# Linear attention, soft mixture of experts and an ELU feed-forward in one kernel: the order and the engines of the weights' conversion, and of the feed-forward's first units, are changed

## The chip, the cores and the metric

The kernel runs on one core of a Trainium2 chip. The metric is the time of one launch in device microseconds (us): the median of repeated runs. The core's engines each work through an instruction queue of their own, in order: TensorE (PE: matrix products; PEld: its weight loads), VectorE (DVE), ScalarE (ACT), GpSimd (POOL) and SyncE (SP, which here only issues DMAs). Where one needs what another makes, it waits on a semaphore.

## The reference

Three layers follow one another. Shapes: batch 4, 8 heads, 768 steps, head size 48; so 3072 tokens of 384 values; 8 experts of 4 slots, hidden size 1024; feed-forward width 2048. `w_in` and `w_out` arrive as 64-bit floating point values; the kernel reads them as pairs of 32-bit words.

```python
for t in range(S):                                   # linear attention, per batch and head
    cur = einsum('bhd,bhe->bhde', u * k_t, v_t)
    y[:, :, t] = einsum('bhd,bhde->bhe', r_t, state + cur)
    state = w * state + einsum('bhd,bhe->bhde', k_t, v_t)
x = y as [3072, 384]
logits = x @ phi                                     # soft mixture of experts
slot_input = softmax(logits over tokens).T @ x
slot_out[e] = relu(slot_input[e] @ w1[e]) @ w2[e]
x = softmax(logits over slots) @ slot_out
h = x @ w_in                                         # feed-forward
out = where(h > 0, h, exp(min(h, 0)) - 1) @ w_out
```

## The kernel before

The program has three stages, and all three engines' orders are those in which the code is written (a manual schedule).

**Attention** works on 24 chunks of 128 tokens (6 per batch), in a loop over s = -2 to 23 in which the pieces of chunks s, s+1 and s+2 are interleaved. For the chunk ahead, `scale` makes `km` (DVE), `turn(0)` transposes r (PE into PSUM tile `ps_r`) and multiplies it by a table into `rT` (DVE), and `turn(1)` transposes `km` into `ps_k`, copies it to `kT` (ACT) and multiplies it by `rT` into `qd` (DVE): this is the "r x k" of the change. `scores` multiplies `kT` by `rT` (PE), `causal` masks the result into two tiles `am` (DVE, line 559), `update` and `state` carry the state forward (`t1` on DVE, then `qc` on POOL, line 583), `bonus_b` ends in `bv` (POOL, line 601), and `rows_b` makes the chunk's output `x` (DVE, line 635), which `x_T` transposes. `ps_r`, `ps_x` and `ps_k` share two PSUM buffers, so `ps_k` waits until DVE has read `ps_r` into `rT`. Pieces of the mixture's logits and slot sums (`part`, `extra`) lie between them, three chunks to a round.

In the same loop the first part of `w_in` and `w_out` is converted from 64 to 32 bits, a piece of 128 x 384 in each of 20 steps (s = 0 to 19): `wide_load` (SP), `wide_a` (two ACT instructions, lines 313 and 314), `wide_b1` (a clamp, line 317, on POOL in this loop), `wide_b2`, `wide_b3`, `wide_c` (DVE, lines 322, 328 and 333), and one step later `wide_d` (two POOL instructions, lines 336 and 337). The loop also issues the loads of the experts' weights (`load_we`), nine of them at a pace set by `(s - 2) * (NWE - 1) // (NP - 3)` (NWE = 10, NP = 20), and one at s = 20 into the buffer of the conversion.

**Experts**: `up`, `turn`, `down` on PE; `turn_c_b` copies the transposed softmax from PSUM to `cT` (12 ACT instructions); `split` cuts five pieces of `w_out` (`wo`) in a rounded part `wh` (ACT) and a remainder `wl` (DVE); `turn_so` and three DVE copies give `sT`.

**Feed-forward**: `through` multiplies `sT` by columns of `w_in` on PE into PSUM tiles `phm`; `through_b` copies half of such a result to `mst` (ACT) and writes the remainder (DVE). Then 48 units (a block of 512 tokens and two columns of 128 hidden values each) run through `hid` (PE, tile `fh`), `tanh` and `expo` (ACT), `neg` and `elu` (DVE), `upper` (ACT, `gh`), `lower` (DVE, `gl`) and `outp` (24 PE products into `fo`). The first four units go in halves (`narrow`).

```python
            wide(s, wide_a)
            wide(s, wide_b1)
...
                rows_b(s)
                wide(s, wide_b2)
                wide(s - 1, wide_d)
...
            wide(s, wide_b3)
            wide(s, wide_c)
            if ahead:
                turn(1, s + 2)
```

Of the kernel before, what the change touches and what calls it, by code (L numbers as in the profile page):

```python
# [236 lines left out]
def kernel(  # L237
# [75 lines left out]
        nc.scalar.activation(out=a.bitcast(F32), in_=raw[:, :, 1].bitcast(F32), func=ACTF.Abs)  # L313
        nc.scalar.activation(out=l.bitcast(F32), in_=l.bitcast(U32), func=ACTF.Copy, scale=2.0 ** -52)

    def wide_b1(raw, a, eng=None):
        (eng or nc.vector).tensor_scalar(  # L317
            out=a.bitcast(F32), in0=a.bitcast(F32), scalar1=EXP_LO, scalar2=EXP_HI, op0=ALU.max, op1=ALU.min
        )

# [76 lines left out]
    with ExitStack() as actx:  # L397
# [415 lines left out]
        def wide(j, f):  # L813
            if 0 <= j < NP:
                raw, a = piece(j)
                if f is wide_b1:
                    f(raw, a, nc.gpsimd)
                    return
                if f is not wide_d:
                    f(raw, a)  # L820
                    return
                merged = []
                for o, at, i, c, p, m in spans(j):
                    if merged and merged[-1][0] == o:
                        merged[-1][3] += m
                    else:
                        merged.append([o, at, p, m])
                for o, at, p, m in merged:
                    wide_d(raw[:, at:at + m, :], a[:, at:at + m], (wov if o else wiv)[:, p:p + m])
# [27 lines left out]
        for s in range(-2, NCH):  # L857
            now, nxt, ahead = s >= 0, 0 <= s + 1 < NCH, s + 2 < NCH
            last = s == NCH - 1
            if nxt:  # L860
                update(s + 1)
            wide(s, wide_a)
            wide(s, wide_b1)
            if last:
                extra()
                extra()
                extra()
                logits(GS - 1, 0, G - 1)
            else:
                extra()  # L870
            if s > 0 and s % G == 0:
                extras += part(s // G - 1)
            if s == -2:
                tables_b()
            if nxt:
                state(s + 1)
            if ahead:
                scale(s + 2)
            if 2 <= s + 4 < NCH:
                load_k(s + 4)  # L880
            if 2 <= s + 3 < NCH:
                load_v(s + 3)
            if s < 1:
                wide_load(s + 2)
            if now:
                for p in range(HP):
                    rows_a(s, p)
                rows_b(s)
                wide(s, wide_b2)
                wide(s - 1, wide_d)  # L890
                if s >= 1 and s + 2 < NP:
                    wide_load(s + 2)
            if nxt:
                for p in range(HP):
                    scores(s + 1, p)
                causal(s + 1)
                bonus_a(s + 1)
                bonus_c(s + 1)
            if not last:
                extra()  # L900
            if ahead:
                turn(0, s + 2)
            if 2 <= s + 4 < NCH:
                load_r(s + 4)
            if nxt:
                for p in range(HP):
                    before(s + 1, p)
            if now:
                x_T(s)
            if last:  # L910
                logits(GS - 1, G - 1, G)
            if nxt:
                bonus_b(s + 1)
            wide(s, wide_b3)
            wide(s, wide_c)
            if ahead:
                turn(1, s + 2)
            if nxt:
                state_b(s + 1)
            if s == NCH - 2:  # L920
                warm(3)
            extra()
            if s >= 2 and (s - 2) * (NWE - 1) // (NP - 3) >= nwe and nwe < NWE - 1:
                load_we(nwe, we_p)
                nwe += 1
            if s == NP:
                assert nwe == NWE - 1
                load_we(nwe, we_p)
                nwe += 1
            if s >= NCH - 3 and not last:  # L930
                h = s - NCH + 3
                (rk_ctx, early)[h].close()
                pool = w2ctx.enter_context(tc.tile_pool(name=f"we2a{h}", bufs=1, side="right", reuse_waits="tile"))
                we.setdefault(NWE, []).append(pool.tile([128, HW], F32, name=f"we2a{h}"))
                load_half(NWE, h)
                nwe = NWE + h
        last_part(GS - 1)
        assert not extras

# [107 lines left out]
    def turn_c_b(b):  # L1047
        ph = ph_p.tile([128, CG // 2, 128], F32, tag="ph", name="phc")
        t = cs.pop(b)
        for i in range(CG // 2):  # L1050
            nc.tensor.transpose(
                out=ph[:, i, :], in_=t[:, 2 * i:2 * i + 2].rearrange("p n a c -> p (n a c)").bitcast(F32), identity=ident
            )
        o = cT[:, 128 * CG * b:128 * CG * (b + 1)].rearrange("p (i n t) -> p i n t", n=2, t=128)
        for n in range(2):
            for a in range(2):
                nc.scalar.copy(out=o[64 * a:64 * a + 64, :, n, :], in_=ph[64 * n:64 * n + 64])


    pt = [po_p.tile([128, 64], F32, tag="po", name="pt") for kk in range(KD)]  # L1060
# [7 lines left out]

    def split(i):
        a, b = (t[:, 2 * i % 8:2 * i % 8 + 2, :] for t in whl[i // 4])  # L1070
        nc.scalar.copy(out=a, in_=wo[:, 2 * i:2 * i + 2, :])
        nc.vector.tensor_tensor(out=b, in0=wo[:, 2 * i:2 * i + 2, :], in1=a.bitcast(F32), op=ALU.subtract)

    up(0)
# [65 lines left out]


    phm = [fo_p.tile([128, 512], F32, tag="fo", name="phm") for _ in range(2)]
    m0 = through(0, 256, phm[0][:, 0:256])
    through_b(*m0, 0)
    m2 = through(1024, 128, phm[0][:, 256:384])
    through_b(*m2, 0)
    through_b(*m2, 1)
    through_b(*m0, 1)


    PB = 384
# [94 lines left out]
    def term(n, i, t, terms):  # L1246
# [1 line left out]
        first, final = (0, FA - 1) if f0 < FA else (FA, FT - 1)  # L1248
        f = f0 + i
        wh, wl = (w[:, f % 8, :] for w in whl[f // 8])  # L1250
        if f == first and 0 in terms:
            po[blk, t] = fo_p.tile([128, DM], F32, tag="fo", name="fo")
        o = po[blk, t]
        s = slice(128 * t, 128 * t + 128)
# [30 lines left out]
    def narrow(n):  # L1285
        u = n - 1
        neg(u, ta)
        if u:
            lower(u - 1, tb)
        elu(u, ta)  # L1290
        if u:
            tanh(n, ta)
        upper(u, ta)
        if not u:
            tanh(n, ta)
        neg(u, tb)
        expo(n, ta)
        lower(u, ta)
        elu(u, tb)
        tanh(n, tb)  # L1300
        upper(u, tb)
        if not u:
            through_b(*m1, 1)
        expo(n, tb)

    late = []
    hid(0)
    m1 = through(512, 256, phm[1][:, 0:256])
    for s in (ta, tb):
        tanh(0, s)  # L1310
        expo(0, s)
    through_b(*m1, 0)
    for n in range(1, N + 3):
        j, at = (n - 7) // 2, n - 2 if n < SHIFT else n - 3
        if n == 2:
# [5 lines left out]
            outp(at, (0,))  # L1321
        if n < N:
            hid(n)
        if n == 20:
            m = through(CA, CB // 2, fh_p.tile([128, 512], F32, tag="fh", name="phm2"))
            late += [(*m, 0), (*m, 1)]
# [77 lines left out]
```

## Time and profile before

| what | value |
|---|---|
| median of 3 runs (lowest, highest) | 467.81 us (466.58, 467.82) |
| the profiled execution | 467.28 us, of which the span of the profile is 465.5 us |
| busy over the span | PE 416.9, DVE 369.6, ACT 268.5, POOL 186.3 us |
| attention, 16.75 to 162.70 us of the span | PE 122.29, DVE 127.69, POOL 102.27 of 145.95 us |
| experts, 180 to 215 us | PE 32.54 of 35 us |
| feed-forward's start, 215 to 235 us | PE 15.83 of 20 us, at a granted clock of 0.83 |
| rest of the feed-forward, 260 to 465 us | PE 193.82 of 205 us |

Busy time alone says little: the four stages have different limits, so each stage is read by itself, by the instructions in order of time and by what ended each wait. Start times are counted from the start of the span. An instruction's row gives its start and its duration; where two of one engine follow without a wait, the second may start a little before the first ends, so that the distance from start to start is what one costs.

### The profile page before, as it was taken

Reading aid. Unit: us, or ns where it says so; the run is one execution under the profiler, and the core shown is the slowest. Engines: PE = TensorE matmul, PEld = TensorE weight load, DVE = VectorE, ACT = ScalarE, POOL = GpSimd, SP = SyncE. Lnnn points to the kernel's source line nnn. Section 1 sums busy time; section 2 is a strip of 40 time slices with the busy share of each in tenths; the row PEclk is TensorE's granted clock in tenths of the full one; section 3 lists DMA queues with packets and bytes.
Section 4 is the critical chain, followed back from the end, with each engine's and each line's share of the span. In section 5 each row is a group of like instructions: output and inputs, shape, how many; then the busy total and the mean of one; then the engine's idle time right before and its main releaser. Section 6 shows DMA issues by size and latency. Waiting matters only on the chain.

```text
span 465.5 us, 9991 instructions
## 1 busy us (share of the span) xinstructions
PE 416.9 (90%) x4009; PEld 365.4 (78%) x4009; DVE 369.6 (79%) x553; ACT 268.5 (58%) x487; POOL 186.3 (40%) x185
## 2 busy tenths in 40 slices
PE   7888788798879898995999899989999999999995
PEld 6777677676768774443899789969998989999994
DVE  4798889898988854454887999996999987787851
ACT  2444254345445332485677787867868686866740
POOL 2385667777777613200000245331234304324440
PEclk9999899999999999998899999999999999999999
DMA  9959989999999858850000111211111001111112
GB/s 127 214 124 273 232 211 252 259 281 261 277 233 244 228 200 271 294 182 0 2 1 0 34 35 35 67 36 35 34 35 34 1 0 51 36 52 68 70 70 73
DMA packets 97575, 57.41 MB, mean 123 GB/s; under 512 B 77808, under 2 KB 89328, under 8 KB 97520
## 3 DMA queue, kind: packets, MB, share of 16 engines
q1 hardware_dynamic: 96704, 56.64, 45.2%
q8 instruction: 33, 0.54, 0.5%
q14 instruction: 22, 0.18, 0.1%
q10 hardware_dynamic: 816, 0.05, 0.1%
HBM read 51.96 MB, written 4.72 MB: 122 GB/s over the span
## 4 chain that ended last, share of the span: by engine, by line
PE 50%; DVE 16%; POOL 13%; ACT 10%; issue 8%; DMA 3%; POOLq 0%; DVEq 0%; ACTq 0%; SPq 0%
PE fo L1256 12%; PE fo L1257 11%; PE fo L1259 11%; POOL scr L317 5%; PE fh L1211 3%; DVE ex L1230 3%; DVE ex L1225 3%; DMA scr<-in_moe_w_out_dram 2%; POOL scr L336 2%; PE ph L1011 2%; POOL bv L601 2%; DVE am L559 2%; ACT scr L313 1%; PE ps_a L554 1%; ACT th L1219 1%
## 5 line engine op out<-in xcount | busy, mean ns | idle before, releaser
L1256 PE MATMUL fo<-wh,gh 128*128 128x384 f32 x384 | 132.3, 344 | 7.0 <-ACT gh L1238 3.7
L1257 PE MATMUL fo<-wl,gh 128*128 128x384 f32 x384 | 130.7, 340 | 0.0
L1259 PE MATMUL fo<-wh,gl 128*128 128x384 f32 x384 | 122.2, 340 | 0.0
L1256 PEld LDWEIGHTS fo<-wh,gh 128*128 128x128 f32 x384 | 72.9, 190 | 14.0 <-ACT acc L1193 6.5
L1225 DVE SCALAR_TENSOR_TENSOR ex<-ex,th 128x1024 f32<-128x1024 f32 (+1 forms) x52 | 62.1, 1195 | 23.3 <-ACT ex L1222 23.1
L336 POOL TENSOR_TENSOR cv<-raw,cv 128x384 f32<-128x384 f32 x12 | 19.8, 1652 | 138.7 <-DVE cv L333 66.4
L1241 DVE TENSOR_TENSOR gl<-ex,gh 128x1024 fp32r<-128x1024 f32 (+1 forms) x52 | 72.0, 1385 | 3.5 <-ACT gh L1238 3.0
L1219 ACT ACTIVATE th<-fh 128x1024 f32<-128x1024 f32 (+1 forms) x53 | 50.3, 949 | 42.4 <-PE fh L1211 42.4
L1257 PEld LDWEIGHTS fo<-wl,gh 128*128 128x128 f32 x384 | 72.8, 190 | 1.9
L1259 PEld LDWEIGHTS fo<-wh,gl 128*128 128x128 f32 x384 | 72.2, 190 | 0.0
L1230 DVE SCALAR_TENSOR_TENSOR ex<-ex,fh 128x1024 f32<-128x1024 f32 (+1 forms) x52 | 58.8, 1131 | 0.1
L1222 ACT ACTIVATE ex<-fh 128x1024 f32<-128x1024 f32 (+1 forms) x53 | 50.3, 949 | 9.5 <-DVE gl L1241 9.4
L1238 ACT CAST gh<-ex 128x1024 fp32r<-128x1024 f32 (+1 forms) x52 | 51.5, 991 | 5.4 <-DVE ex L1230 4.2
L1198 POOL TENSOR_TENSOR acc<-os,acc 128x384 f32<-128x384 f32 x20 | 29.0, 1482 | 49.7 <-ACT os L1197 49.7
L317 POOL TENSOR_SCALAR scr<-scr 128x384 f32<-128x384 f32 x20 | 30.8, 1538 | 35.7 <-ACT scr L313 35.7
L522 PE MATMUL ps_k<-ident,km 128*128 128x128 f32 x96 | 15.9, 290 | 23.5 <-DVE rT L532 22.2
L646 ACT COPY xT<-ps_x 128x384 f32<-128x384 f32 x24 | 11.5, 479 | 38.6 <-PE ps_x L644 38.6
L1211 PE MATMUL fh<-cT,mst 128*128 128x512 f32 x96 | 31.0, 404 | 2.8 <-DVE ex L1230 2.8
L522 PEld LDWEIGHTS ps_k<-ident,km 128*128 128x128 f32 x96 | 10.4, 143 | 28.4 <-DVE rT L532 26.7
L527 ACT COPY kT<-ps_k 128x512 f32<-128x512 f32 x24 | 14.1, 587 | 30.4 <-PE ps_k L522 30.2
L559 DVE TENSOR_TENSOR am<-ps_a,mask 128x512 f32<-128x512 f32 x48 | 30.7, 678 | 0.9 <-PE ps_a L554 0.9
L554 PE MATMUL ps_a<-rT,kT 64*128 64x128 f32 x384 | 29.0, 292 | 0.6 <-DVE rT L532 0.6
(160 smaller groups left out, 729.0 us busy)
## 6 DMA issues: line engine op xcount, KB each, us to landing
we<-in_moe_w_dram SPq DMA_DIRECT2D x14, 768.0 KB, 7.6
we<-in_moe_w_dram SPq DMA_DIRECT2D x16, 512.0 KB, 6.4
rp<-in_r_dram SPq DMA_DIRECT2D x24, 192.0 KB, 4.7
rk<-in_k_dram SPq DMA_DIRECT2D x24, 192.0 KB, 4.9
vd<-in_v_dram SPq DMA_DIRECT2D x24, 192.0 KB, 5.2
out_dram<-acc SPq DMA_DIRECT2D x24, 192.0 KB, 1.9
we<-in_moe_w_dram SPq DMA_DIRECT2D x16, 256.0 KB, 6.0
scr<-in_moe_w_out_dram SPq DMA_DIRECT2D x10, 384.0 KB, 5.1
```

The source lines that it names most:

```text
L317: (eng or nc.vector).tensor_scalar(out=a.bitcast(F32), in0=a.bitcast(F32), scalar1=EXP_LO, scalar2=EXP_HI, op0=ALU.max, op1=ALU.min)
L559: nc.vector.tensor_tensor(out=am[n, a], in0=aps[a], in1=mask.unsqueeze(1).to_broadcast([128, HP, 128]), op=ALU.mult)
L1211: nc.tensor.matmul(out=ph[n][:, i, :], lhsT=mst[(f + i) // 8][:, 128 * ((f + i) % 8):128 * ((f + i) % 8) + 128], rhs=cT[:, TB * blk:TB * b ...
L1219: nc.scalar.activation(out=th[n][:, s], in_=ph[n][:, s], func=ACTF.Tanh, scale=0.5)
L1222: nc.scalar.activation(out=ex[n][:, s], in_=ph[n][:, s], func=ACTF.Exp)
L1225: nc.vector.scalar_tensor_tensor(out=ex[n][:, s], in0=ex[n][:, s], scalar=1.0, in1=th[n][:, s], op0=ALU.add, op1=ALU.mult)
L1230: nc.vector.scalar_tensor_tensor(out=ex[n][:, s], in0=ex[n][:, s], scalar=0.0, in1=ph[n][:, s], op0=ALU.min, op1=ALU.max)
L1238: nc.scalar.copy(out=gh[n][:, s], in_=ex[n][:, s])
L1241: nc.vector.tensor_tensor(out=gl[n][:, s], in0=ex[n][:, s], in1=gh[n][:, s].bitcast(F32), op=ALU.subtract)
L1256: nc.tensor.matmul(out=o, lhsT=gh[n][:, i, s], rhs=wh, start=(f == first), stop=False)
L1257: nc.tensor.matmul(out=o, lhsT=gh[n][:, i, s], rhs=wl, start=False, stop=False)
L1259: nc.tensor.matmul(out=o, lhsT=gl[n][:, i, s], rhs=wh, start=False, stop=(f == final))
```

## The change

1. In the attention loop `wide_b1` (the clamp) goes from POOL to DVE and stands where `wide_b2` stood, behind `x`; `wide_b2` goes behind `bonus_b`, `turn(1)` (with `qd`) comes next, and `wide_b3` and `wide_c` follow it.
2. The loads of the experts' weights are paced over 20 steps instead of 17, the last one a step later.
3. In the experts' stage half of the `cT` copies go from ACT to DVE, and the `wh` copies from ACT to POOL.
4. At the feed-forward's start the first two `through` results lie in different PSUM tiles, `through_b` of the third comes later, one of its halves between DVE's instructions for unit 0, and 12 products of 128 x 384, whose result is overwritten, are added on PE ahead of the first `fo`.

```diff
-    def wide_b1(raw, a, eng=None):
-        (eng or nc.vector).tensor_scalar(
+    def wide_b1(raw, a):
+        nc.vector.tensor_scalar(
...
-                if f is wide_b1:
-                    f(raw, a, nc.gpsimd)
-                    return
...
             wide(s, wide_a)
-            wide(s, wide_b1)
...
                 rows_b(s)
-                wide(s, wide_b2)
+                wide(s, wide_b1)
                 wide(s - 1, wide_d)
...
                 bonus_b(s + 1)
+            wide(s, wide_b2)
+            if ahead:
+                turn(1, s + 2)
             wide(s, wide_b3)
             wide(s, wide_c)
-            if ahead:
-                turn(1, s + 2)
...
-            if s >= 2 and (s - 2) * (NWE - 1) // (NP - 3) >= nwe and nwe < NWE - 1:
+            if s >= 2 and (s - 2) * (NWE - 1) // NP >= nwe and nwe < NWE - 1:
...
-            if s == NP:
-                assert nwe == NWE - 1
-                load_we(nwe, we_p)
-                nwe += 1
+            if s == NP + 1:
+                load_we(NWE - 1, we_p)
...
-                nc.scalar.copy(out=o[64 * a:64 * a + 64, :, n, :], in_=ph[64 * n:64 * n + 64])
+                (nc.vector.tensor_copy if n else nc.scalar.copy)(
+                    out=o[64 * a:64 * a + 64, :, n, :], in_=ph[64 * n:64 * n + 64]
+                )
...
-        nc.scalar.copy(out=a, in_=wo[:, 2 * i:2 * i + 2, :])
+        nc.gpsimd.tensor_copy(out=a, in_=wo[:, 2 * i:2 * i + 2, :])
...
-    m0 = through(0, 256, phm[0][:, 0:256])
-    through_b(*m0, 0)
-    m2 = through(1024, 128, phm[0][:, 256:384])
-    through_b(*m2, 0)
-    through_b(*m2, 1)
-    through_b(*m0, 1)
+    m0 = through(0, 256, phm[1][:, 0:256])
+    m2 = through(1024, 128, phm[0][:, 0:128])
+    for i in range(2):
+        through_b(*m0, i)
+    for i in range(2):
+        through_b(*m2, i)
...
         neg(u, tb)
+        if not u:
+            through_b(*m1, 0)
         expo(n, ta)
...
-    m1 = through(512, 256, phm[1][:, 0:256])
+    m1 = through(512, 256, phm[1][:, 256:512])
...
-    through_b(*m1, 0)
...
+        if n == 1:
+
+            po[0, 0] = fo_p.tile([128, DM], F32, tag="fo", name="fo")
+            for i in range(12):
+                nc.tensor.matmul(
+                    out=po[0, 0], lhsT=whl[0][0][:, 0, :128], rhs=whl[0][0][:, 0, :], start=True, stop=True
+                )
```

How the instructions stand on DVE in one chunk of the attention loop, before:

```order
L635 TENSOR_TENSOR x<-py,bv 128x384
L322 TENSOR_SCALAR scr<-scr 128x384
L559 TENSOR_TENSOR am<-ps_a,mask 128x512 x2
L532 TENSOR_TENSOR rT<-ps_r,vt 128x512
L328 SCALAR_TENSOR_TENSOR scr<-scr 128x384
L333 TENSOR_SCALAR scr<-scr 128x384
L529 TENSOR_TENSOR qd<-rT,ps_k 128x512
```

and now:

```order
L635 TENSOR_TENSOR x<-py,bv 128x384
L317 TENSOR_SCALAR scr<-scr 128x384
L559 TENSOR_TENSOR am<-ps_a,mask 128x512 x2
L532 TENSOR_TENSOR rT<-ps_r,vt 128x512
L322 TENSOR_SCALAR scr<-scr 128x384
L529 TENSOR_TENSOR qd<-rT,ps_k 128x512
L328 SCALAR_TENSOR_TENSOR scr<-scr 128x384
L333 TENSOR_SCALAR scr<-scr 128x384
```

The clamp (L317) has taken the place of `wide_b2` (L322), which now stands between `rT` and `qd`; L328 and L333 have gone from ahead of `qd` to behind it.

POOL in one chunk, before:

```order
L317 TENSOR_SCALAR scr<-scr 128x384
L583 TENSOR_TENSOR qc<-t_149,w_141 128x192
L336 TENSOR_TENSOR scr<-scr 128x384
L337 TENSOR_TENSOR wo<-scr 128x384
L601 TENSOR_TENSOR bv<-vd,bs 128x384
```

and now:

```order
L583 TENSOR_TENSOR qc<-t_149,w_141 128x192
L336 TENSOR_TENSOR scr<-scr 128x384
L337 TENSOR_TENSOR wo<-scr 128x384
L601 TENSOR_TENSOR bv<-vd,bs 128x384
L583 TENSOR_TENSOR qc<-t_149,w_141 128x192
```

POOL's next instruction behind `bv` is now `qc`, which waits for DVE's `t1`; L336 and L337 (of the piece before) follow it at once.

DVE where the feed-forward starts, before:

```order
L1105 COPY sT<-pt 128x64 x3
L1139 TENSOR_TENSOR mst_3166<-phm,mst_3166 64x256
L1139 TENSOR_TENSOR mst_3167<-phm,mst_3167 64x128 x2
L1139 TENSOR_TENSOR mst_3166<-phm,mst_3166 64x256 x2
L1225 SCALAR_TENSOR_TENSOR ex<-ex,th 128x512
L1230 SCALAR_TENSOR_TENSOR ex<-ex,fh 128x512
L1225 SCALAR_TENSOR_TENSOR ex<-ex,th 128x512
L1241 TENSOR_TENSOR gl<-ex,gh 128x512
```

and now (its lines have moved by two):

```order
L1103 COPY sT<-pt 128x64 x3
L1137 TENSOR_TENSOR mst_3166<-phm,mst_3166 64x256 x2
L1137 TENSOR_TENSOR mst_3167<-phm,mst_3167 64x128 x2
L1223 SCALAR_TENSOR_TENSOR ex<-ex,th 128x512
L1228 SCALAR_TENSOR_TENSOR ex<-ex,fh 128x512
L1223 SCALAR_TENSOR_TENSOR ex<-ex,th 128x512
L1137 TENSOR_TENSOR mst_3166<-phm,mst_3166 64x256
L1239 TENSOR_TENSOR gl<-ex,gh 128x512
```

The third `through`'s first subtraction has gone from ahead of the first `neg` (L1225, now L1223) to behind the second one, ahead of `lower` (`gl`).

## Rows read from the trace of the kernel before

**Rows 1.** Busy time by stretch: start:end, us, then PE, PEld, DVE, ACT, POOL, PEclk, DMA share, GB/s
```profile
16.75:162.70 145.95, 122.29 (x2083) 103.36 (x2082) 127.69 (x242) 65.45 (x188) 102.27 (x100) 0.99 0.95 238
```

**Rows 2.** Waits of DVE, 16 to 163 us: total us, times, longest
```profile
DVE scr L322 <- POOL scr L317: 11.0, 10, 1.6
```

**Rows 3.** Order of time, DVE and POOL, one chunk: start us, us, engine, line
```profile
130.40 1.02 POOL L336 TENSOR_TENSOR scr<-scr 128x384 f32<-128x384 f32 x1
130.47 1.17 DVE L322 TENSOR_SCALAR scr<-scr 128x384 int32<-128x384 int32 x1 [1.32 <-POOL scr L317]
131.56 1.28 DVE L559 TENSOR_TENSOR am<-ps_a,mask 128x512 f32<-128x512 f32 x2
...
132.75 0.68 DVE L532 TENSOR_TENSOR rT<-ps_r,vt 128x512 f32<-128x512 f32 x1
133.35 0.54 DVE L328 SCALAR_TENSOR_TENSOR scr<-scr 128x384 int32<-128x384 int32 x1
...
133.93 0.36 DVE L333 TENSOR_SCALAR scr<-scr 128x384 int32<-128x384 int32 x1
...
134.85 0.69 DVE L529 TENSOR_TENSOR qd<-rT,ps_k 128x512 f32<-128x512 f32 x1 [0.56 <-ACT kT L527]
...
136.82 0.51 POOL L583 TENSOR_TENSOR qc<-t,w 128x192 f32<-128x192 f32 x1
136.89 0.65 DVE L322 TENSOR_SCALAR scr<-scr 128x384 int32<-128x384 int32 x1
```

**Rows 4.** Order of time, step s = 20: no clamp, but L336 follows `qc`
```profile
155.49 0.35 DVE L582 TENSOR_TENSOR t<-qc,pu 128x192 f32<-128x192 f32 x1
...
155.98 0.69 POOL L583 TENSOR_TENSOR qc<-t,w 128x192 f32<-128x192 f32 x1 [1.42 <-ACT c_sb L702]
156.22 0.55 DVE L635 TENSOR_TENSOR x<-py,bv 128x384 f32<-128x384 f32 x1
...
156.63 1.02 POOL L336 TENSOR_TENSOR scr<-scr 128x384 f32<-128x384 f32 x1
156.72 1.29 DVE L559 TENSOR_TENSOR am<-ps_a,mask 128x512 f32<-128x512 f32 x2
```

**Rows 5.** Order of time, DVE: output `x` of chunk 1
```profile
23.69 0.55 DVE L635 TENSOR_TENSOR x<-py,bv 128x384 f32<-128x384 f32 x1
```

**Rows 6.** Order of time, DVE in the feed-forward: the clamp on DVE, POOL idle
```profile
263.64 0.35 DVE L317 TENSOR_SCALAR cv<-cv 128x384 f32<-128x384 f32 x1
```

**Rows 7.** Order of time, end of the experts' stage; last row: POOL's clamp, ns min/median/max
```profile
204.60 1.80 PE L1033 MATMUL pd<-we,h1T 128*32 128x384 f32 x20
...
205.44 1.56 ACT L1071 CAST wh<-wo 128x768 fp32r<-128x768 f32 x2
...
207.03 0.58 ACT L1037 ACTIVATE so<-pd,rz 128x384 f32<-128x384 f32 x1
L317 POOL TENSOR_SCALAR scr<-scr x20: 1487/1505/1750, 16.7 to 149.3; 128x384 f32<-128x384 f32 x20
```

**Rows 8.** Order of time, feed-forward's start
```profile
212.32 0.26 ACT L1138 CAST mst<-phm 64x128 fp32r<-64x128 f32 x1 [1.43 <-PE phm L1129]
...
213.94 0.60 ACT L1219 ACTIVATE th<-fh 128x512 f32<-128x512 f32 x1
...
216.27 0.42 DVE L1139 TENSOR_TENSOR mst<-phm,mst 64x256 fp32r<-64x256 f32 x1 [1.90 <-ACT mst L1138]
216.72 0.69 DVE L1225 SCALAR_TENSOR_TENSOR ex<-ex,th 128x512 f32<-128x512 f32 x1
...
228.32 0.63 PE L1211 MATMUL fh<-cT,mst 128*128 128x512 f32 x2
```

**Rows 9.** Busy time by stretch in the feed-forward, columns as in rows 1
```profile
222.00:224.00 2.00, 2.00 (x7) 1.81 (x6) 1.97 (x4) 0.90 (x2) 0.00 (x0) 0.50 0.00 0
...
226.00:228.00 2.00, 2.00 (x14) 2.00 (x13) 1.91 (x4) 0.79 (x2) 0.00 (x0) 1.00 0.02 4
260.00:465.00 205.00, 193.82 (x1060) 184.91 (x1058) 172.28 (x171) 140.86 (x181) 69.27 (x43) 1.00 0.13 43
```

More of the change, by code (lines that the diff above doesn't have):

```diff
@@ L936 @@
                 nwe = NWE + h
+        assert nwe == NWE + 1
         last_part(GS - 1)
@@ L1250, in term @@
         wh, wl = (w[:, f % 8, :] for w in whl[f // 8])
-        if f == first and 0 in terms:
+        if f == first and 0 in terms and (blk, t) not in po:
             po[blk, t] = fo_p.tile([128, DM], F32, tag="fo", name="fo")
```

## The prediction

> **What bounds the kernel now.** I read the busy time by stretch first, to see which stages have one limit; then, stage by stage, the waits and the instructions in order of time. In the attention loop DVE is busy 127.69 of 145.95 us, ahead of PE and POOL [rows 1]. So 18.3 us of DVE are idle there, and 11.0 of these are waits of `wide_b2` (L322) for the clamp on POOL (L317) [rows 2]. What a chunk costs is a ring through DVE: `x`, L322, two `am`, `rT`; then PE's `ps_k` and ACT's `kT`; then `qd` and on to the next `x`. From the start of `rT` to the start of `qd` are 2.10 us (132.75 to 134.85), and L328 and L333 lie inside them: they cost nothing there, since `qd` would wait for `kT` anyway (0.56 us it still does) [rows 3]. The chunks' `x` come from 23.69 us (s = 1) [rows 5] to 156.22 us (s = 20) [rows 4]: 19 chunks of 6.98 us.
>
> One thing more is to be seen in rows 3. L322 takes 1.17 us where POOL's L336 started 0.07 us before it, and ends 0.22 us after L336 does; beside the short `qc`, which also started 0.07 us earlier, it takes 0.65. The same kind of instruction takes 0.35 us with POOL idle [rows 6]. So these DVE instructions wait until the POOL instruction that came first has ended. The Trainium skill says why on the page "SBUF — State Buffer", section "Who interferes with whom": DVE's two-port modes and GpSimd share a port pair, whoever issues first has it for the whole instruction, the other blocks. That speaks against giving DVE one more instruction of this kind; the trace agrees with it, by the 1.17 us.
>
> In the feed-forward PE is the limit, 193.82 of 205 us [rows 9], so a delay or a gain at its start lasts to the end.
>
> **The change, part by part**, against the profiled execution's 467.28 us (span 465.5 us; 0.5 us under the median of the runs).
>
> *Attention, per chunk.* L328 and L333 leave the 2.10 us, where they were free, and come behind `qd`: 0.58 us (133.35 to 133.93) and 0.36, in sum 0.94 us on the ring [rows 3]. POOL should be idle then, so I take the undisturbed durations. L322 goes into the 2.10 us in their place and costs nothing; were it to wait out a whole POOL instruction, as it waits out L336's 1.02 us in rows 3, it would still fit into the 1.5 us between the end of `rT` and `qd`. That takes off what it cost: 0.57 us beside `qc` in 16 chunks (0.65 less an overlap of 0.08), 1.09 beside L336 in 4 (130.47 to 131.56): 0.67 in the mean [rows 3]. The wait for POOL's clamp goes too: 11.0 us / 19 = 0.58 [rows 2].
>
> The clamp on DVE stands behind `x`. What does it meet? POOL's next work is `qc`, released by `t1`, and L336 at once behind it. Step s = 20 shows that order, without a clamp: `t1` starts at 155.49, `qc` 155.98, L336 at 156.63, and the DVE instruction behind `x` at 156.72 [rows 4]. The clamp would start there: 0.09 us behind L336, as L322 did with 0.07. So bounds for it are 0.35 us [rows 6] and 1.17 (1.09 from start to start) [rows 3], and I take 1.09, whose row has the same neighbours in the same order.
>
> Sum: 0.94 + 1.09 - 0.67 - 0.58 = +0.78 us a chunk. In 3 of the 19 chunks (the last but one of a batch, which have no `qc`) POOL begins earlier, and the clamp waits for L337's end instead: some 0.45 less each. 19 x 0.78 - 1.35 = 13.5 us. Of DVE's 18.3 us idle, 7.3 are not in the term of 11.0 [rows 1, 2]; some hang on POOL's clamp as well, and I let 3 of them go: **+10.5 us**. The 30 us that POOL loses (20 x 1.5 [rows 7]) gain nothing beyond the wait already counted.
>
> *Pace of the loads.* The queue is as full in bytes as before; two of the ten expert weights come a step or two later, and those are read by `down` only, which has all of `up` on PE before it. Cost nothing; without that cover one load of 1.57 MB at 238 GB/s [rows 1] would be 6.6 us.
>
> *Experts.* PE is continuous up to the end of `down(1)`, 204.60 + 1.80 = 206.40. ACT's `so`, which reads it, starts at 207.03, because two `wh` copies end at 207.00 [rows 7]. With the copies on POOL, `so` starts some 0.07 us behind PE: **-0.55 us**. POOL's price for a copy of 768 columns isn't shown. ACT's 0.78 is one end; twice the clamp's 1.5 us for 384 columns, 3.0, is the other [rows 7]. I take 1.5, nearer ACT's, since a copy has no arithmetic. Five are 7.5 us, and POOL has them all behind `up(1)`, 14 us ahead of `sT`: hidden at either end but for 1 us at the upper, where the last `wl` would come late for `sT`. The six `cT` copies that go to DVE lie beside PE's `down(1)`, where DVE has only `wl` to make; uncovered they would cost about six copies of the size of `so`, 6 x 0.58 = 3.5 us [rows 7].
>
> *Feed-forward's start.* ACT waits 1.43 us for PE's second `through` at 212.32, which waited until the first was read from the same PSUM tile, and the first `tanh` starts at 213.94 [rows 8]. In two tiles that wait goes, and `tanh` should start near 212.7, 1.2 us earlier. The first `neg` at 216.72 stood behind the third `through`'s subtraction at 216.27 [rows 8], and not behind `expo`; freed, it starts near 213.9, 2.8 us earlier. But that subtraction, 0.42 us and the wait for its ACT copy, now lies between `neg` and `lower`: it gives back about 1.2, and DVE's chain is 1.6 us earlier from there. Then the clock: it stood at 0.50 in 222 to 224, PE's 1.2 GHz level, and 7 products ran in 2 us; at the upper level 14 do [rows 9]. The 12 added products fill PE's empty time ahead of the first `fo`; at the upper level they take 1.7 us and end about when `gh` is there. If the clock holds, the 7 products to 224 cost 1 us instead of 2, and `hid` of unit 3 (228.32) comes 1.6 + 1.0 = 2.6 us earlier: **-2.6 us**. Ends: 0 (clock falls anyway, added products in the way) and -4.
>
> Sum: 467.3 + 10.5 - 0.55 - 2.6 = 474.6; I say **474.5 us**.
>
> **The rivals.** *The clamp comes first (faster).* If it has the port before L336, it costs 0.34 instead of 1.09 in the 16 chunks with `qc`: 16 x 0.75 = 12 us less, 462.5 us. The point that decides is the 0.09 us between L336 and the clamp [rows 4]. For it: it is small, and 0.69 us of `qc` there has slack in it (0.51 in rows 3). Against it: in rows 3 POOL won with 0.07 us, twice. The Trainium skill, page "Perfetto Trace Analysis", section "GPSIMD Engine Instruction", warns that a GpSimd span in a profile isn't reliable and that start-to-start spacing should be used; if so, when L336 takes the port is less sure than its row, and this rival would give its 462.5. The spacing agrees with the rows here (`qc` to L336, 0.65). *It is mixed:* the clamp wins in about half of the chunks, 474.5 - 6 = 468.5. *The feed-forward gives nothing:* the added products delay the first `fo`, or the clock falls in the gap behind it (PE should still wait there, for `gl` of unit 0): 477. For it: the clock did fall after an idle stretch in this place [rows 9].
>
> **How the numbers follow.** Forecast 0.52 (474.5), clamp first 0.27 (462.5), mixed 0.10 (468.5), no gain in the feed-forward 0.11 (477). Its own range, by the ends of -4 and 0 and by 3 us either way for the idle time that I let go: 471 to 478. Cases of both signs hold most of the chance, so the range goes on to the faster rival: 460.5 to 478. A measurement of this kernel tells 0.3%, 1.4 us, from no change. Faster: clamp first and a quarter of the mixed, 0.30. Same: 0.05. Slower: 0.65.
>
> **What would show it.** In the changed profile: chunk-to-chunk distance of `x` near 7.5 us (6.98 before), L317 on DVE at 1.1 to 1.2 us with L336 starting just before it, L322 hidden, L328 and L333 at 0.54 and 0.36; no DVE wait for POOL. `so` right behind `down(1)`; the clock at its upper level from `hid(0)` on; the distance from the first `tanh` to the end shorter by 1 to 2 us. Wrong if L317 on DVE has 0.35 us in most chunks (the first rival), or if the ring breaks elsewhere: L322 longer than the time for `kT`, or L328 and L333 made longer by a POOL instruction beside them.

## The result, and the profile after

The changed kernel takes 460.44 us (median of 4 runs, 458.81 to 462.65) against 467.19 of the kernel before in the same session: a ratio of 0.986, with an interval of 0.983 to 0.990. It is 1.4% faster; 474.5 us and slower was the forecast.

Where the 7.5 us between the two profiled executions (467.28 and 459.78 us; 7.4 of them inside the spans) lie is read from the start times of a few instructions:

| stretch | before | after | difference | forecast |
|---|---|---|---|---|
| start to `x` of s = 0 | 16.75 | 15.46 | -1.29 | 0 |
| 20 chunks, `x` of s = 0 to s = 20 | 139.47 | 135.83 | -3.64 | +10.5 |
| on to the first `sT` (last chunks, experts) | 51.97 | 51.75 | -0.22 | -0.55 |
| `sT` to `hid` of unit 3 | 20.13 | 17.99 | -2.14 | -2.6 |
| `hid` of unit 3 to the end of the span | 237.18 | 237.07 | -0.11 | 0 |

The experts and the feed-forward came out about as forecast; the attention loop went the other way, and the start moved, of which the forecast had nothing. Its busy times, in the columns of [rows 1], for the stretch that answers to them:

```profile
15.46:158.13 142.67, 126.15 (x2086) 103.52 (x2085) 127.64 (x263) 64.92 (x188) 72.48 (x80) 0.99 0.96 245
```

DVE has as much to do as before, 127.64 us, but in 3.3 us less (both stretches end with `x` of s = 21); the wait for POOL's clamp [rows 2] is gone. Now the waits, of DVE and then of PE (total us, times, longest), in the loop after:

```profile
DVE qd L529 <- ACT kT L527: 13.4, 17, 1.7
...
PE ps_k L522 <- ACT xT L646: 6.4, 14, 0.5
PE ps_k L522 <- DVE rT L532: 5.1, 6, 1.3
```

and PE's largest before:

```profile
PE ps_k L522 <- DVE rT L532: 22.2, 19, 2.3
```

Here is the surprise. Before, `ps_k` (the transpose of `k`, `turn(1)`) waited for DVE's `rT` in 19 chunks. After, it waits in 14 chunks for ACT's copy `xT` instead. By its data it needs neither. It waits for the reader of whatever last lay in its PSUM buffer. `ps_r`, `ps_k` and `ps_x` come from one pool, `pt_p`, with two buffers, and nothing in the code says which of the two a tile gets. In the program of before, `ps_k` follows `ps_r` in its buffer in 21 of the 23 chunks whose buffer held another tile before, and `ps_x` in one; in that of the change it follows `ps_x` in 14 and `ps_r` in 8. The lines that allocate these tiles are untouched: the assignment moved along with the order of the code.

One chunk of the change with `ps_x`'s buffer, in order of time (start us, us, engine, line):

```profile
102.96 0.55 DVE L635 TENSOR_TENSOR x<-py,bv 128x384 f32<-128x384 f32 x1
...
103.37 1.01 POOL L336 TENSOR_TENSOR scr<-scr 128x384 f32<-128x384 f32 x1
103.43 1.17 DVE L317 TENSOR_SCALAR scr<-scr 128x384 f32<-128x384 f32 x1
...
103.66 1.10 PE L612 MATMUL py<-qb,rT 128*128 128x96 f32 x8 [0.59 <-ACT bt L572]
...
104.59 0.49 PE L644 MATMUL ps_x<-ident,x 128*128 128x128 f32 x3
...
105.12 0.48 ACT L646 COPY xT<-ps_x 128x384 f32<-128x384 f32 x1 [1.04 <-PE ps_x L644]
...
105.66 0.66 PE L522 MATMUL ps_k<-ident,km 128*128 128x128 f32 x4 [0.46 <-ACT xT L646]
105.72 0.67 DVE L532 TENSOR_TENSOR rT<-ps_r,vt 128x512 f32<-128x512 f32 x1
...
106.32 0.48 DVE L322 TENSOR_SCALAR scr<-scr 128x384 int32<-128x384 int32 x1
106.40 0.59 ACT L527 COPY kT<-ps_k 128x512 f32<-128x512 f32 x1 [0.73 <-PE ps_k L522]
...
107.02 0.69 DVE L529 TENSOR_TENSOR qd<-rT,ps_k 128x512 f32<-128x512 f32 x1 [0.23 <-ACT kT L527]
...
107.63 0.55 DVE L328 SCALAR_TENSOR_TENSOR scr<-scr 128x384 int32<-128x384 int32 x1
...
108.21 0.36 DVE L333 TENSOR_SCALAR scr<-scr 128x384 int32<-128x384 int32 x1
...
109.39 0.55 DVE L635 TENSOR_TENSOR x<-py,bv 128x384 f32<-128x384 f32 x1
```

`ps_k` starts 0.06 us ahead of `rT`, and `rT` to `qd` is 1.30 us. The next chunk of the same trace has `ps_r`'s buffer:

```profile
112.15 0.67 DVE L532 TENSOR_TENSOR rT<-ps_r,vt 128x512 f32<-128x512 f32 x1
...
112.88 0.66 PE L522 MATMUL ps_k<-ident,km 128*128 128x128 f32 x4 [1.00 <-DVE rT L532]
...
113.63 0.59 ACT L527 COPY kT<-ps_k 128x512 f32<-128x512 f32 x1 [1.27 <-PE ps_k L522]
...
114.25 0.69 DVE L529 TENSOR_TENSOR qd<-rT,ps_k 128x512 f32<-128x512 f32 x1 [0.77 <-ACT kT L527]
...
117.10 0.55 DVE L635 TENSOR_TENSOR x<-py,bv 128x384 f32<-128x384 f32 x1
```

There `ps_k` waits 1.00 us for `rT`, and `rT` to `qd` is the 2.10 us of [rows 3]. The first chunk took 6.43 us from `x` to `x`, this one 7.71. Much else of the forecast is in the rows of the first chunk: the clamp starts 0.06 us behind L336 and takes 1.17 us (so it does in 11 of 20 chunks), L322 is hidden, L328 and L333 have 0.55 and 0.36.

For the experiments a chunk is cut in two: from the start of `x` to that of `qd`, where PE and ACT work beside DVE, and from `qd` to the next `x`, where L328 and L333 now stand. Sums over 20 chunks (s = 0 to 20), from the start times of `x` and `qd`, with DVE's busy time and the mean granted clock over the same stretch:

| kernel | `ps_k` shares with | `x` to `qd` | `qd` to `x` | sum, us | DVE busy | clock |
|---|---|---|---|---|---|---|
| before | `ps_r` in 21 of 23 | 104.68 | 34.79 | 139.47 | 123.22 | 0.99 |
| the change | `ps_x` in 14 of 23 | 84.50 | 51.33 | 135.83 | 123.11 | 0.99 |
| e1 the change | `ps_r` | 93.73 | 51.45 | 145.18 | 123.36 | 0.96 |
| e2 the change | `ps_x` | 81.81 | 51.33 | 133.14 | 123.14 | 1.00 |
| e3 before | `ps_x` | 99.09 | 34.62 | 133.71 | 120.45 | 0.99 |
| e4 e2, clamp early | `ps_x` | 87.96 | 62.53 | 150.49 | 113.66 | 0.91 |
| e5 e2, all steps behind `rT` | `ps_x` | 93.59 | 33.05 | 126.64 | 123.62 | 1.00 |
| e6 e5, clamp on POOL | `ps_x` | 104.54 | 32.76 | 137.30 | 133.97 | 1.00 |
| e9 e1, L328 and L333 put back | `ps_r` | 98.33 | 33.72 | 132.05 | 126.93 | 0.97 |
| e10 e1, clamp on POOL | `ps_r` | 82.11 | 56.00 | 138.11 | 116.88 | 0.96 |

### The profile page after: what moved, and what is told of

Same layout as the page of the kernel before. It is cut to its first block, busy times and chain, and to the rows that moved or that the text cites. A ratio compares the mean times of both kernels' runs of the same rounds, so it can differ in the third digit from the quotient of the medians.

```text
span 458.1 us, 10069 instructions
## 1 busy us (share of the span) xinstructions
PE 419.4 (92%) x4021; PEld 363.8 (79%) x4021; DVE 373.4 (82%) x579; ACT 260.7 (57%) x476; POOL 160.2 (35%) x170
## 4 chain that ended last, share of the span: by engine, by line
PE 61%; DVE 21%; issue 7%; ACT 7%; DMA 2%; SPq 1%; DVEq 0%; ACTq 0%
PE fo L1254 11%; PE fo L1257 11%; PE fo L1255 11%; PE fh L1209 3%; DVE ex L1228 3%; PE py L612 3%; PE ps_a L554 3%; DVE ex L1223 3%; PE ps_k L522 3%; PE py L625 3%; PE pd L1029 2%; PE ph L1007 2%; DVE am L559 2%; DVE km L517 2%; DVE scr L317 2%
## 5 line engine op out<-in xcount | busy, mean ns | idle before, releaser
L1223 DVE SCALAR_TENSOR_TENSOR ex<-ex,th 128x1024 f32<-128x1024 f32 (+1 forms) x52 | 62.1, 1194 | 24.1 <-ACT ex L1220 23.9
L336 POOL TENSOR_TENSOR cv<-raw,cv 128x384 f32<-128x384 f32 x12 | 19.5, 1624 | 132.3 <-DVE cv L333 59.8
L583 POOL TENSOR_TENSOR qc<-t,w 128x192 f32<-128x192 f32 x20 | 14.5, 723 | 59.9 <-DVE t L582 21.7
L529 DVE TENSOR_TENSOR qd<-rT,ps_k 128x512 f32<-128x512 f32 x24 | 16.5, 686 | 16.0 <-ACT kT L527 16.0
L554 PE MATMUL ps_a<-rT,kT 64*128 64x128 f32 x384 | 27.9, 285 | 0.3 <-ACT kT L527 0.2
L625 PE MATMUL py<-vd,am 128*64 128x48 f32 x768 | 27.3, 226 | 0.0
```

Of the source, the lines that this page charges most:

```text
L554: nc.tensor.matmul(out=aps[a][:, p, :], lhsT=kT[q, p, :], rhs=rT[n][q, p, :], start=True, stop=True)
L625: nc.tensor.matmul(out=py[q:q + 64, h, :], lhsT=am[n, a][:, p, q:q + 64], rhs=vd[n][:, h, :], start=(c == 0), stop=(c == 0 or h == H - 1),)
L1223: nc.vector.scalar_tensor_tensor(out=ex[n][:, s], in0=ex[n][:, s], scalar=1.0, in1=th[n][:, s], op0=ALU.add, op1=ALU.mult)
```

## The experiments

Theory A: the change gained because `ps_k` changed its buffer. Rival B: the new order gains whichever buffer `ps_k` has.

**e1, e2, e3: the buffer alone.** The first two are the change, the third is the kernel before. The edit of e1 leaves one buffer to `ps_r` and `ps_k`, and another to `ps_x`; e2 and e3 give `ps_k` the tag `px` too (tiles of one tag share a set of buffers).

```diff
-        pt_p = actx.enter_context(tc.tile_pool(name="pt_p", bufs=2, space=PSUM))
+        pt_p = actx.enter_context(tc.tile_pool(name="pt_p", bufs=1, space=PSUM))
...
-            ps = pt_p.tile([128, KD, 128], F32, tag="pt", name="ps_x")
+            ps = pt_p.tile([128, KD, 128], F32, tag="px", name="ps_x")
```

> The changed kernel with one edit: ps_r and ps_k share one PSUM buffer in every chunk (before the edit they do so in about 9 chunks of 23). Theory A (the change gained because ps_k got the bank of ps_x in 14 chunks, so that it no longer waited for rT): every chunk is then one of the 7.05 to 7.7 us kind instead of 14 of the 6.4 to 6.7 us kind, rT to qd is 2.1 us everywhere, and 14 x 0.8 us come back: 470 to 473 us. Rival B (the later steps' place behind r x k is what gains, whichever bank ps_k has): 459 to 462 us.

> The changed kernel with one edit: ps_k shares its PSUM buffer with ps_x in every chunk, so never waits for rT. Theory A: the 9 or so chunks that are left at 7.05 to 7.7 us fall to 6.4 to 6.7 us, 9 x 0.6 to 0.8 us less: 453 to 456 us, and no wait of ps_k for VectorE is left in the attention stage. Rival B: no change, 459 to 462 us. If the weight loads bound the stage (DMA share .96 of it), also no change, with x waiting for its transfer.

> The kernel before, with the one edit that ps_k shares its PSUM buffer with ps_x in every chunk. Theory A in its strong form (the bank alone is the gain): the 2 us between rT and qd fall to 1.3 us in each chunk, 458 to 460 us. Theory A in its weaker form (the freed 0.8 us is only there when the two later steps are out of that gap, since they take 0.9 us of VectorE in it): qd's own wait for kT goes, about 2 us in all, 464.5 to 466.5 us. Rival B: 467 us.

Measured: e1 473.09 us, 1.015 of before (1.012 to 1.018); e2 458.85 us, 0.985 (0.982 to 0.988); e3 461.63 us, 0.991 (0.988 to 0.994). PE's waits in e1 and then in e2:

```profile
PE ps_k L522 <- DVE rT L532: 20.0, 18, 2.6
```

```profile
PE ps_k L522 <- ACT xT L646: 10.1, 22, 0.5
```

Rival B falls with e1: the same instructions in the same order, with the buffer that `ps_k` had before, are slower than before. e1 lies 0.1 us above theory A's 470 to 473. Between e1 and e2 only the buffer differs, 14.2 us: in the traces e2 is 12.0 us shorter in the loop, 2.3 in the start, where e1 makes `ps_k` wait for `rT` from the first chunk on (the kernel before doesn't), and 1.5 behind `sT`, where the clock fell in e1, but 1.2 longer from s = 20 to `sT`. In e1's loop `ps_r` waits for no reader of `ps_k`, so that its new neighbour costs it nothing there. e2 gained less on the change than theory A said: 458.85 us is not in its 453 to 456, but just under rival B's 459. Of the 20 chunks counted, six have `ps_r`'s buffer in the change, and not nine; four of them give 0.5 to 1.1 us, two nothing. That is 2.7 us in the loop (135.83 to 133.14), 1.0 of it lost again in a later start; the two times can't be told apart. e3 lies between its two forms and gained more than the 2 us of the weaker one, 5.8 us in the loop: 2.5 of them between `rT` and `qd` (sums of 41.55 and 39.00), the rest ahead of `rT`, where the wait for POOL's clamp fell from 11.0 us to 8.9; why that fell wasn't followed up.

**e4: the clamp ahead of the state's instructions**, where POOL is idle, on e2:

```diff
+            wide(s, wide_b1)
             if nxt:
                 state(s + 1)
...
                 rows_b(s)
-                wide(s, wide_b1)
```

> As the run with ps_k behind ps_x, and the clamp of VectorE issued ahead of the state's instructions, where GpSimd is idle, so that it doesn't stand behind the sum on GpSimd. If the clamp's 1.17 us is the shared port's doing, it takes 0.35 us there, 0.5 to 0.8 us of each of 20 chunks less on VectorE: 443 to 450 us if VectorE still sets the chunk, and 451 to 456 us if TensorE (5.9 us of a chunk) or the loads do. If the clamp waits there for ScalarE's absolute value, the gain is smaller by that wait.

Measured: 477.16 us, 1.023 (1.019 to 1.027): 18 us slower than e2, though the clamp takes 0.35 us. In order of time:

```profile
115.13 0.55 DVE L635 TENSOR_TENSOR x<-py,bv 128x384 f32<-128x384 f32 x1
...
115.82 1.10 PE L612 MATMUL py<-qb,rT 128*128 128x96 f32 x8 [1.61 <-DVE x L635]
...
117.82 0.44 PE L522 MATMUL ps_k<-ident,km 128*128 128x128 f32 x2 [0.46 <-ACT xT L646]
...
119.19 0.69 DVE L529 TENSOR_TENSOR qd<-rT,ps_k 128x512 f32<-128x512 f32 x1 [1.32 <-ACT kT L527]
...
120.82 0.35 DVE L317 TENSOR_SCALAR scr<-scr 128x384 f32<-128x384 f32 x1
...
121.82 0.55 DVE L635 TENSOR_TENSOR x<-py,bv 128x384 f32<-128x384 f32 x1
```

In this chunk and in ten others `x` to `qd` is 4.05 to 4.07 us, as in most chunks of e2 and in the chunk of the change above: `x` frees `py`, then come L612, `ps_x`, `xT`, `ps_k` and `kT`, on PE and ACT. The long clamp stood beside that and cost nothing; the short one stands in `qd` to `x`, where DVE alone sets the pace, and there it also waits for ACT's absolute value (4.8 us in 7 chunks). Against e2 `qd` to `x` grows by 11.2 us in the 20 chunks. All cases of the expectation were gains; only the wait that it names at the end was there. The granted clock fell as well, to 0.83 in the mean from 40 to 80 us, where three chunks have 5.4 to 5.7 us from `x` to `qd`, and `x` to `qd` grows by 6.2 us in all; so the 18 us aren't the clamp's alone.

**e5, e6: all four DVE steps between `rT` and `qd`**, on e2 (the cut is e5's); in e6 the clamp stays where the change has it in the code, but on POOL, so behind `qc`:

```diff
                 rows_b(s)
-                wide(s, wide_b1)
...
+            wide(s, wide_b1)
             wide(s, wide_b2)
+            wide(s, wide_b3)
+            wide(s, wide_c)
             if ahead:
                 turn(1, s + 2)
-            wide(s, wide_b3)
-            wide(s, wide_c)
```

> ps_k in ps_x's bank in every chunk, and all of the conversion's VectorE steps (clamp and the three after it) between rT and qd. With that bank x to qd takes 4.06 us whatever VectorE does, because TensorE and ScalarE set it (x, state rows, ps_x, xT, ps_k, kT), and the two steps behind qd (0.91 us) lie in the other part, qd to x, which VectorE sets. Theory A (the chunk is these two parts in a row): x to qd stays at 4.1 to 4.3 us, qd to x falls from 2.36 to 1.45 us in a plain chunk, and 10 to 18 us of 20 chunks go unless TensorE's own sum (6.0 us of a chunk) ends it: 443 to 451 us. Rival C (the chunk is bound by the sum of VectorE's work, or by the loads at a DMA share of 1.0): 455 to 460 us.

> As the run with all steps between rT and qd, with the clamp on GpSimd, where it was before the change. Theory A: VectorE has slack between x and qd either way, so within 2 us of that run, unless bv comes late behind the clamp on GpSimd. Rival C (VectorE's sum): 20 clamps less on VectorE, 7 us faster than that run.

Measured: e5 455.95 us, 0.979 (0.975 to 0.982); e6 462.54 us, 0.991 (0.988 to 0.994). `qd` to `x` fell to 1.5 us in most chunks of e5, as expected, but `x` to `qd` rose to 4.55:

```profile
99.67 0.68 DVE L532 TENSOR_TENSOR rT<-ps_r,vt 128x512 f32<-128x512 f32 x1
...
100.27 0.48 DVE L317 TENSOR_SCALAR scr<-scr 128x384 f32<-128x384 f32 x1
...
100.78 0.36 DVE L322 TENSOR_SCALAR scr<-scr 128x384 int32<-128x384 int32 x1
100.79 1.04 POOL L601 TENSOR_TENSOR bv<-vd,bs 128x384 f32<-128x384 f32 x1 [0.26 <-ACT bs L596]
101.18 1.07 DVE L328 SCALAR_TENSOR_TENSOR scr<-scr 128x384 int32<-128x384 int32 x1
...
102.28 0.36 DVE L333 TENSOR_SCALAR scr<-scr 128x384 int32<-128x384 int32 x1
102.56 0.68 DVE L529 TENSOR_TENSOR qd<-rT,ps_k 128x512 f32<-128x512 f32 x1
```

L328 takes 1.07 us beside POOL's `bv` and ends 0.42 behind it; alone it takes 0.55. The Trainium skill, page "SBUF — State Buffer", section "Who interferes with whom", says that a DVE instruction with two inputs in SBUF, as L328 is, contends with a GpSimd instruction that reads SBUF; the trace agrees, by the 1.07 us. In e6 POOL's work behind the clamp moves along, and three DVE steps meet it one after another:

```profile
106.38 1.01 POOL L336 TENSOR_TENSOR scr<-scr 128x384 f32<-128x384 f32 x1
106.77 0.84 DVE L322 TENSOR_SCALAR scr<-scr 128x384 int32<-128x384 int32 x1
...
107.47 1.02 POOL L337 TENSOR_TENSOR wo<-scr 128x384 f32<-128x384 f32 x1
107.70 1.21 DVE L328 SCALAR_TENSOR_TENSOR scr<-scr 128x384 int32<-128x384 int32 x1
...
108.46 1.14 POOL L601 TENSOR_TENSOR bv<-vd,bs 128x384 f32<-128x384 f32 x1
108.95 0.87 DVE L333 TENSOR_SCALAR scr<-scr 128x384 int32<-128x384 int32 x1
```

So `rT` to `qd` is 3.55 us in most chunks of e6, and it is slower than e5 though DVE has 20 instructions less. Both expected figures for e6 were wrong (within 2 us of e5; 7 us faster); theory A's exception names a late `bv`, but what the rows show is DVE held up beside POOL. e5's 455.95 us lies in rival C's range and not in theory A's 443 to 451. e6 refutes what rival C gave for it, but not that DVE's sum is the limit: counted with the time that its instructions lose to POOL, DVE is busy 123.62 of 126.64 us in e5's loop and 133.97 of 137.30 in e6's, idle for 3 us in each, where e2 leaves 10.0.

**e9, e10: the two terms of the loop apart**, on e1. e9 puts L328 and L333 back ahead of `turn(1)`; e10 puts the clamp back on POOL.

> ps_k in ps_r's bank in every chunk (the run at 473 us), with the two later steps (L328, L333) put back ahead of qd, behind L322; the clamp stays on VectorE behind x. The prediction's term of 0.94 us for these two: if they fit beside L322 in the 2.1 us from rT to qd (0.36 to 0.5 + 0.55 + 0.36 us behind rT's 0.68), qd to x falls by 0.9 us and x to qd stays at 4.86, 14 to 18 us less of 20 chunks: 455 to 459 us. If they don't fit, or bv on GpSimd lengthens them, x to qd grows and the gain is half of it: 464 us or more.

> ps_k in ps_r's bank in every chunk (the run at 473 us), with the clamp back on GpSimd behind qc and the other steps as the change has them. This takes the clamp out of the way from x to rT. The prediction's term of 1.09 us less the chunks where it took 0.35: x to qd falls from 4.86 to about 4.0 us in the chunks where the clamp stood behind the sum, 8 to 14 us less: 459 to 465 us. If L322 then waits for GpSimd's clamp and the two sums behind it, as in the run with the late clamp on GpSimd, x to qd stays near 4.9 to 5.2 us: 472 to 476 us.

Measured: e9 458.88 us, 0.983 (0.980 to 0.987); e10 464.51 us, 0.994 (0.991 to 0.997). Both lie in the range expected, e10 at its upper end. With `ps_r`'s buffer throughout, moving L328 and L333 behind `qd` cost 13.1 us of the loop (132.05 to 145.18), and the clamp's move with L322's gave 7.4 (139.47 to 132.05). Neither sum is clean: e9's trace is of an execution of 462.21 us, 3.3 over its median, with the granted clock at 0.50 from 36.4 to 43.0 us, where s = 2 and 3 take 8.55 and 7.74 us. e10's chunks are mostly 3.77 us from `x` to `qd`, but three intervals of 8.4 to 9.1 us lie in it, beside 3.7 us in which PE waits for `vd` and a clock of 0.50 from 35.4 to 38.6 and from 96.8 to 103.4 us; so it gives no price of the clamp. e9 with the old buffer takes what e2 takes with the new one: leaving L328 and L333 ahead of `qd` was worth as much as the buffer.

**e7, e8, e12: the feed-forward's start undone, the 12 added products removed, the experts' copies undone**, each alone on the change.

> The changed kernel with the feed-forward's start as it was before (order of the first hidden units, added products away). If the reordering gave the 2.1 us by which the first hidden unit comes earlier behind the experts: 462 to 463 us. If that was the clock's or chance: 460.4 us.

> The changed kernel without the 12 added products alone. If they are what keeps the granted clock at 1.00 from 200 to 236 us (0.50 in a part of it before): the clock falls there and 0.5 to 1.5 us come on, 461 to 462 us. If the reordering alone holds the clock, or the products only fill idle time: 460.4 us, the same clock.

> The changed kernel with the experts' copies as before (all cT and wh copies on ScalarE). If the copies on ScalarE are what held so back: so starts 0.5 to 0.6 us behind the end of down(1) again (0.07 us now), and from the last x to sT it is 0.5 to 0.6 us longer; the whole time within 1 us of 460.4. If the gain there came from elsewhere: no change of that distance.

Measured: e7 461.36 us, 0.988 (0.985 to 0.991); e8 459.58 us, 0.984 (0.981 to 0.987); e12 461.22 us, one run. The intervals of e7 and e8 overlap with the change's, and e12 has none, so the distances within the traces decide. From `sT` to `hid` of unit 3: 20.31 us in e7, 17.98 in e8, 17.99 in the change. With the order undone it is 2.3 us longer, without the products the same. In e12 `so` starts at 202.51, behind two `wh` copies on ACT that began at 200.92: 0.64 us behind the end of `down(1)` (201.87), against 0.07 in the change; from `x` of s = 23 to `sT` it takes 34.01 us, the change 33.44, as expected. Without the products the clock did fall, here in e8:

```profile
212.00:214.00 2.00, 1.68 (x7) 1.16 (x6) 1.69 (x3) 1.16 (x3) 0.00 (x0) 0.56 0.04 8
```

and in e1, with the products, it fell later:

```profile
229.00:231.00 2.00, 2.00 (x8) 2.00 (x8) 1.92 (x4) 1.62 (x4) 0.00 (x0) 0.50 0.00 0
```

In e8 that cost nothing: around this stretch PE waits 3.0 us for ACT's `gh` and DVE's `gl`. In e1 PE is busy throughout, and `sT` to `hid` takes 19.53 us, 1.5 more. So the products don't hold the clock by themselves: it fell in e1, e6, e9 and e10, and not in the change, e2, e4, e5, e11 and e12, which all have the same feed-forward; why, no run tells.

**e11: e5 with three loads of expert weights moved to the last three steps.**

> The fastest version so far (all steps between rT and qd, ps_k in ps_x's bank), with three of the ten expert weights' loads moved to the last three steps. If its last chunks wait for their inputs because the queue is full (vd waits 3.6 us there, two intervals of 7.6 to 8.0 us), those fall to 6.3 us and 3 to 4 us go: 452 to 453 us. If the experts then wait for the moved loads, or the wait only moves there: 456 us or more.

Measured: 454.50 us, 0.973 (0.970 to 0.976), the fastest kernel here, though its interval overlaps e5's; it lies between the two cases expected. e5 gives back part of its loop behind s = 20: from there to `sT` it takes 55.85 us, the change 51.75, with two intervals of 7.98 and 7.63 us. In e11 these are 6.70 and 5.59, but two intervals of 7.9 us come up at 85 to 100 us, beside waits for `vd`: the wait mostly moved. The DMA share is 0.99 to 1.01 in the loops of e5 and e11, so the loads may be the next limit, or DVE with its 3 us idle in e5; no run parts the two.

## Why the prediction was wrong

**The step that failed** is the sentence "From the start of `rT` to the start of `qd` are 2.10 us", taken for a property of the ring: "`rT`; then PE's `ps_k` and ACT's `kT`; then `qd`". The step from `rT` to `ps_k` is not a dependency of data but the reuse of a PSUM buffer, and the change moved that. The kernel's description says that three kinds of tiles share two buffers, "so `ps_k` waits until DVE has read `ps_r`"; that holds only where `ps_k` follows `ps_r`. The rivals were about the shared port and the feed-forward, none about the buffer. In the loop the buffer is worth -9.4 us (145.18 in e1, 135.83 in the change); with it held, the change costs +5.7 (139.47 to 145.18): slower, as forecast, but half of the +10.5.

e1's ratio of 1.015 makes 474.4 us of the profiled 467.28, which is the forecast's 474.5. That is luck. In the traces e1 is 6.1 us longer than before, and 2.0 of these are its later start, which the forecast didn't have. By halves of the chunk e1 has +16.6 us in `qd` to `x` (forecast 0.94 in 19 chunks, 17.9) and -10.9 in `x` to `qd` (forecast -7.4).

- *L328 and L333, 0.94 us a chunk.* Right in place and near in size: the +16.6 us are 0.83 a chunk; from e9 to e1 it is 0.89. That they cost nothing ahead of `qd` holds for the kernel before, where `rT` to `qd` is 2.10 us in 19 of 20 chunks. In e9, with L322 in the same gap, `x` to `qd` is 4.6 us longer than in e1: 1.3 of it is the chunk s = 3 at the lower clock, and in nine chunks L328 or L333 meets `bv` and takes up to 1.21 or 0.87 us.
- *The clamp and L322.* +1.09 - 0.67 - 0.58, less the 1.35 and the 3 us let go, is -7.4 us in the loop; e9 against before shows -7.4 too, but with a lower clock in e9 and with a term that is off, and no run has each part alone. In the change the clamp waits out L336 in 11 of the 16 chunks with `qc` and L336, as forecast (1.17 us, L336 0.05 to 0.06 us ahead), and the end of POOL's instruction in the three without `qc` (0.64 to 0.70). In the other five it has the port and takes 0.34 or 0.35, as the first rival said of most, so that the "mixed" one (468.5 us) is nearest in this. In e1 `x` to `qd` is 4.03 to 4.53 us in these five and 4.86 in most others: 3.2 us in all, nearly the 3.5 by which -10.9 goes beyond -7.4. Two of the five, in the change:

```profile
55.90 1.28 POOL L336 TENSOR_TENSOR scr<-scr 128x384 f32<-128x384 f32 x1
55.96 0.34 DVE L317 TENSOR_SCALAR scr<-scr 128x384 f32<-128x384 f32 x1
...
76.80 0.34 DVE L317 TENSOR_SCALAR scr<-scr 128x384 f32<-128x384 f32 x1
...
76.85 1.18 POOL L336 TENSOR_TENSOR scr<-scr 128x384 f32<-128x384 f32 x1
```

  At 76.80 the clamp comes first, and L336 takes 1.18 us instead of 1.01. At 55.96 L336's row starts 0.06 us ahead, as where it wins, and still it is L336 that is longer, 1.28: the rows' order doesn't tell the winner in each chunk, the doubt that the prediction names for this rival. Its 462.5 us came near for another reason: in the chunks with `ps_x`'s buffer it doesn't matter who wins. In e2 `x` to `qd` is 4.06 us in the five chunks with the short clamp and 4.07 or less in eight of the 11 with the long one.
- *Experts, -0.55.* `so` starts right behind `down(1)`:

```profile
199.69 2.12 PE L1029 MATMUL pd<-we,h1T 128*32 128x384 f32 x24
...
201.88 0.58 ACT L1033 ACTIVATE so<-pd,rz 128x384 f32<-128x384 f32 x1 [3.40 <-PE pd L1029]
...
203.04 0.67 DVE L1103 COPY sT<-pt 128x64 f32<-128x64 f32 x3 [1.06 <-PE pt L1062]
```

  From `x` of s = 23 to `sT` are 33.44 us, 34.00 before: -0.56, and e12 gives it back. POOL's copies were hidden.
- *Feed-forward, -2.6.* It is -2.14. The rows that answer to [rows 8]:

```profile
207.69 0.60 ACT L1217 ACTIVATE th<-fh 128x512 f32<-128x512 f32 x1
...
208.80 0.69 DVE L1223 SCALAR_TENSOR_TENSOR ex<-ex,th 128x512 f32<-128x512 f32 x1 [0.81 <-ACT ex L1220]
...
221.03 0.62 PE L1209 MATMUL fh<-cT,mst 128*128 128x512 f32 x2
```

  `th` stands 4.65 us behind `sT` (5.75 before), the first `neg` 5.76 (8.53): 1.1 and 2.8 us earlier, 1.2 and 2.8 forecast. The products' part was wrong: e8 has the same distance without them. The clock's part isn't separated from that of DVE's chain, but the traces bound it. From `sT` to `hid` of unit 3, with the mean granted clock between them, the old order takes 20.13 us (before, 0.83), 20.31 (e7, 0.83) and 19.43 (e3, 0.91); the new one 17.99 (the change) and 18.00 (e2), both at 1.00, 17.98 (e8, 0.91), but 19.31 to 19.53 in e1, e6, e9 and e10 (0.91), where PE works through the fall with few gaps or none. So at 0.91 the new order can cost what the old one does, and the 2.14 us were there only where the clock stayed up or fell beside a gap.
- *Pace of the loads, 0.* No run has it alone.
- *The start, 0.* `x` of s = 0 comes 1.29 us earlier. The granted clock from 9 to 16 us is 1.00 in the change, e3 and e5 (`x` at 15.46 to 15.48), and 0.76 and 0.78 in before and e2 (16.75 and 16.45). Since e2 has the change's order, these 1.29 us can't be put down to the change; why the clock falls stays open. e10 starts later still at a clock of 1.00 (17.55), and e1 at 0.76 (18.73): there `ps_k` has `ps_r`'s buffer from the first chunk on and waits for `rT` twice, for 0.9 to 1.0 us.

## What to carry to other kernels

Before a wait is used as a fixed piece of a ring, ask whether it is data or the reuse of a buffer: if tiles of several kinds rotate through one pool, an edit of the order alone can change which wait is there, and a tag for each kind takes the chance out of it. Cut a chunk into the part where other engines set the pace and the part where one engine does; an instruction made longer may be free in the first, and one made shorter may cost in the second, as the clamp did in e4. Here the other buffer alone took 5.8 us off the loop of before (e3), more than the change's 3.6, and another order with the old buffer 7.4 (e9); the fastest versions, e5 and e11, have both, and no run has their order with the old buffer.

## What the runs showed of the hardware

- The clamp isn't the only DVE instruction that is longer beside POOL: in e6 L322, L328 and L333 take 0.84, 1.21 and 0.87 us, where they take 0.35, 0.55 and 0.36 alone. Where DVE and POOL start 0.05 to 0.06 us apart, the one that loses the port is longer (the clamp 1.17 instead of 0.35, or L336 1.18 to 1.28 instead of 1.01). The two `am`, which read PSUM, are not lengthened: in the change they take 1.28 us beside L336 and 1.27 with POOL idle.

```profile
77.07 1.28 DVE L559 TENSOR_TENSOR am<-ps_a,mask 128x512 f32<-128x512 f32 x2
...
84.48 1.27 DVE L559 TENSOR_TENSOR am<-ps_a,mask 128x512 f32<-128x512 f32 x2
```

- A fall of the granted clock to 0.50 behind a stretch in which PE waited cost 1.5 us where PE had work without gaps (e1) and nothing where it had not (e8).
- POOL's `wh` copy of 768 columns, which had no row before, takes 0.83 us: less than the 1.5 us that its clamp needs for 384.
